# Linear attention, then a MoE layer, then a noisy top-2 MoE: the order of GpSimd's work in the attention is written out, low parts of weights are spread, and weight pieces are loaded sooner

## The chip, the cores and the metric

One core of one Trainium2 chip. The time is the device time of one launch in microseconds (us), as the median of several runs. The core has five engines that run beside each other and meet at semaphores: TensorE (PE, with its weight loads shown as PEld), VectorE (DVE), ScalarE (ACT), GpSimd (POOL) and SyncE (SP), whose queue issues nearly all DMAs here.

## The reference

Three layers in a row, all in float32 results:

```python
# attention: q, k, v of (4 batches, 8 heads, 576 tokens, 64), w_phi (64, 128)
phi(x) = concat[exp(p), exp(-p)],  p = x @ w_phi - max|x @ w_phi| per token
kv = phi(k)^T v ; z = sum over tokens of phi(k)
x  = (phi(q) @ kv) / (phi(q) @ z + 1e-6)          # -> (2304 tokens, 512)
# first MoE: w1, w2, w3 (512, 768), w_out (768, 512)
x  = max(x@w1, x@w2, x@w3) @ w_out
# second MoE: 8 experts, w1 (8, 512, 1024), w2 (8, 1024, 512)
noisy logits = x@w_gate + log(1+exp(x@w_noise)) * noise ; top 2 per token, softmax over the two
out[token] += weight * (relu(x[token] @ w1[e]) @ w2[e])
```

The weights of the first MoE arrive as 64-bit floats. The kernel turns their bits into float32 itself.

## The kernel before, in words

**The attention** runs over 16 steps s: a pair of heads of one batch each. Its work is a pipeline over periods a = 2 to 15 (function `period`), which holds three steps at once: step a is turned (transposed on PE), projected with w_phi, and its peaks and centers are made on DVE and its exponentials on ACT; step a-1 has kv_sum (PE, L525), z_sum (L544, with the key sums `zs`) and the turn of centered q; step a-2 has its denominator (PE L585, ACT `dn` L593, DVE turns and reciprocals L600 to L617) and its numerators (L570), which DVE divides into xT (L623). Even periods carry the 64 remaining tokens per head too (turn and projection "r").

**The key tiles**: `z_add(s)` on POOL adds the four tiles of the exponentials of k in three additions (zt twice, L534; zs, L535). z_sum on PE reads zs in the next period.

**The pieces**: the 64-bit weights of the first MoE are cut into 24 pieces of 512 KB (`halves`: group g = 0 to 2, matrix j, half c). Each period from a = 1 to 15 treats one piece (0 to 14); the others follow after the attention. A piece goes through:

- `narrow_load`: DMA of the bits on SP (L194) into a buffer `bits`, of which there are two
- `narrow_mid`: DVE takes the high word apart (L205, a tensor_scalar; L214, a scalar_tensor_tensor with two inputs), ACT makes the low word a number (L216); the result is `nm`
- `narrow_end`: ACT takes the absolute value (L224), POOL adds the low word to `nm` as integers (L225) and, for groups 0 and 1, masks tiny values (L228, L229); group 2 is masked on DVE in `narrow_mask` (L236)
- `narrow_out`: group 0 is split into a high part (ACT, L252) and a low part (L253, POOL for group 0, DVE for group 2), which the products of the first MoE read; group 1 is stored to DRAM (L247) and read again later (L258)

**What sets the order.** Every step is put on a plan with a due time (`at(t, f, ...)`, in units of about a us; a period is STEP = 10.9, the attention ends at T = 16 STEP), and the plan is run in the order of the times. For PE, ACT, DVE and SP this order is the order in the engine's queue. For POOL it is not: there the tile framework's scheduler orders the instructions by its own costs, unless an instruction is tied to the one before it by `in_order`. In the attention before the change nothing on POOL is tied.

**After the attention** the first MoE runs over 6 chunks of 384 tokens (PE L857 first products, L884 second), with the late pieces converted beside chunk 0; then routing, and the experts.

Of the kernel before, what the change touches and what calls it, by code (L numbers as in the profile page):

```python
# [9 lines left out]
F32 = mybir.dt.float32  # L10
F32R = mybir.dt.float32r
BF16 = mybir.dt.bfloat16
I32 = mybir.dt.int32
U32 = mybir.dt.uint32
AF = mybir.ActivationFunctionType
ALU = mybir.AluOpType
# [3 lines left out]
P = 128  # L20
TINY = 1.125 * 2.0 ** -15


class Plan:
# [5 lines left out]
    def at(self, t, f, *x):  # L30
        self.ops.append((t, len(self.ops), f, x))
# [7 lines left out]
def tile_linear_attention__then__moe__then__noisy_top2_moe(  # L39
# [20 lines left out]
    nc = tc.nc  # L60
# [30 lines left out]
    at = plan.at  # L91
    st, pools = {}, {}
# [36 lines left out]
    def split(hi, lo, src):  # L129
        nc.scalar.activation(hi, src, AF.Copy)  # L130
        nc.vector.tensor_tensor(lo, src, hi.bitcast(F32), op=ALU.subtract)  # L131

    xT = big.tile([P, KD, N], F32, name="xT", tag="big")

    def raw_tile():
# [5 lines left out]
    def ring(i):  # L141
        pool, n = (ring_a, 4) if i % 12 < 4 else (pools["ring_b"], 8)
        return tuple(pool.tile([P, 1024], F32R, name=nm, bufs=n) for nm in ("wh", "wl"))
# [5 lines left out]
    def block(ws, g, j):  # L149
        w = ws[j]  # L150
        if j < 3:
            return w[:, g * 256:(g + 1) * 256].rearrange("(a p) f -> p a f", p=P)
        return w[g * 256:(g + 1) * 256, :].rearrange("(a p) f -> p a f", p=P)

    def half(ap_, j, c):
        n = ap_.shape[1] // 2
        return ap_[:, c * n:(c + 1) * n, :]
# [5 lines left out]
    halves = [(g, j, c) for g in range(NG) for j in range(4) for c in range(2)]  # L163

    def direct(g, j):
        return g != 1
# [34 lines left out]
    def narrow_high(n):  # L201
        if ("bits", n) not in st:
            return
        m_ = pools["m2" if "m2" in pools else "attn"].tile([P, 512], I32, name="nm", tag="x2", bufs=3)
        nc.vector.tensor_scalar(m_, st["bits", n][:, :, 1], 0x07ffffff, 3, op0=ALU.bitwise_and,  # L205
                                op1=ALU.logical_shift_left)
        st["nh", n] = m_

    def narrow_low(n):
# [6 lines left out]
        nc.scalar.activation(low, low.bitcast(U32), AF.Copy, scale=float(2.0 ** -29))  # L216
        st["nm", n] = m_

    def narrow_end(n):
        if ("nm", n) not in st:  # L220
            return
        m_, bits = st["nm", n], st["bits", n]
        high = bits[:, :, 1].bitcast(F32)
        nc.scalar.activation(high, high, AF.Abs)  # L224
        nc.gpsimd.tensor_tensor(m_, m_, bits[:, :, 0], op=ALU.add)  # L225
        if halves[n][0] < 2:
            g_, o_ = bits[:, :, 0].bitcast(F32), m_.bitcast(F32)
            nc.gpsimd.tensor_scalar(g_, high, TINY, None, op0=ALU.is_ge)  # L228
            nc.gpsimd.tensor_tensor(o_, o_, g_, op=ALU.mult)  # L229

    def narrow_mask(n):
        if ("nm", n) not in st:
            return
        o_, bits = st.pop(("nm", n)).bitcast(F32), st.pop(("bits", n))
        if halves[n][0] == 2:
            nc.vector.scalar_tensor_tensor(o_, bits[:, :, 1].bitcast(F32), TINY, o_, op0=ALU.is_ge,  # L236
                                           op1=ALU.mult)
        st["nf", n] = o_

    def narrow_out(n):  # L240
        g, j, c = halves[n]
        if ("nf", n) not in st:
            return
        o_ = st.pop(("nf", n))
        if not direct(g, j):
            dst = half(block(narrow, g, j), j, c)
            dq.dma_start(dst, o_.rearrange("p (a f) -> p a f", a=dst.shape[1]))  # L247
            return
        if c == 0:
            W1[g, j] = ring(4 * g + j)  # L250
        hi, lo = (w[:, c * 512:(c + 1) * 512] for w in W1[g, j])
        nc.scalar.activation(hi, o_, AF.Copy)  # L252
        (nc.vector if g else nc.gpsimd).tensor_tensor(lo, o_, hi.bitcast(F32), op=ALU.subtract)  # L253

    def w1_load(g, j):
        src = block(narrow, g, j)
# [140 lines left out]
    kps, qps = {}, {}  # L397
# [131 lines left out]
    def z_add(s):  # L529
        t = ap.tile([P, 2, 2, 2, NF], F32, name="zt")  # L530
        z = ap.tile([P, 2, 2, NF], F32, name="zs")
        for h in range(2):
            hs = slice(2 * h, 2 * h + 2)
            nc.gpsimd.tensor_tensor(t[:, h], kps[s][:, 0, hs], kps[s][:, 1, hs], op=ALU.add)  # L534
        nc.gpsimd.tensor_tensor(z, t[:, :, 0], t[:, :, 1], op=ALU.add)  # L535
        st["zs", s] = z

    def z_sum(s):
# [87 lines left out]
    NS = B * HP  # L626
    STEP = 10.9
# [35 lines left out]
    def step_halves(a):  # L663

        def count(a):
            return min(a, 1)

        n = sum(count(i) for i in range(a))
        return range(n, n + count(a) if a < NS else len(halves))
# [14 lines left out]
            at(t + backs[n] + 0.5, divide, c, n)  # L684

    def narrow_steps(n, at, *times):
        for t, f in zip(times, (narrow_load, narrow_mid, narrow_end, narrow_mask, narrow_out)):
            at(t, f, n)

    def loads(a, at):  # L690
        if 0 < a < NS:
            at(0.0, fill, a)
            if a == 3:
                at(3.0, routing_loads)
            if a == 2:
                at(2.0, routing_consts)
            if a + 1 < NS:
                if a > 1:
                    at(0.0, load_main, a + 1)
                at(0.0, load_vals, a + 1)  # L700
            if a + 1 == 2 * HP:
                at(0.0, load_rest, 1)
        if a == 2 * HP:
            at(7.5, load_rest_v, 1)
        if a < NS:
            for n in step_halves(a):
                narrow_steps(n, at, 5.0, 9.9, 12.25, 16.5, 21.5)

    def period(a):
        base = a * STEP  # L710
# [2 lines left out]
        def at(t, f, *x):  # L713
            plan.at(base + t, f, *x)
# [28 lines left out]
        if even:  # L743
# [3 lines left out]
                at(4.83 + 0.01 * g, center, a, "r", g)  # L747
            for sg in range(2):
                at(9.5, exp_k, a, "r", 0, sg)
        at(7.6, z_add, a)  # L750
        both(7.4, "q", a, at)
        at(4.6, kv_sum, b)
        at(6.8, z_sum, b)
# [66 lines left out]
    T = NS * STEP  # L820
# [105 lines left out]
    def small(shape, name, dt=F32, bufs=2):  # L926
        return pools["work"].tile(shape, dt, name=name, bufs=bufs)

    scat = []

    def in_order(ins, but=()):

        if st["loop"]:
            return
        names = {o.ins.name for o in but}
        for i in reversed(nc.cur_bb.bb.instructions):
            if i.engine == ins.ins.engine and i is not ins.ins and i.name not in names:
                tc.add_manual_dep(ins.ins, i.name,
                                  mybir.DependencyInfo(mybir.DependencyClass.NoSync,
                                                       mybir.DependencyReason.DATA))  # L940
                return

    st["loop"] = False

    def route(c):

# [583 lines left out]
    END = clock[0] + 1.9  # L1530
    at(END, open_rest)
    at(END + 1.6, routing_split)
    late_ones = step_halves(NS)
    narrow_steps(late_ones[0], at, T - 4.0, T + 4.0, T + 5.5, T + 10.0, T + 11.5)
    for i, n in enumerate(late_ones[1:]):
        t = END + 2.0 + 2.6 * i
        narrow_steps(n, at, END + (0.01 * i if i < 5 else 2.6 * i - 1.0), t, t + 2.65, t + 5.0, t + 6.0)
    for i, (g, j) in enumerate(((1, 0), (1, 1), (1, 2), (1, 3))):
        t = END + 0.1 + i * 2.6
        at(max(t - 6.3, T + 9.0) if i < 2 else max(t - 6.3, END + 0.06), w1_load, g, j)  # L1540
# [64 lines left out]
    for c in range(NCHUNK):  # L1605
        if c == 1:
            for i, job in enumerate(jobs):
                t = clock[0] + 8.0 * i
# [55 lines left out]
    for n, (e, M, row0) in enumerate(units):  # L1664
# [9 lines left out]
        if seven(n):  # L1674
            for two in ((0, 1), (2, 3)):
                for q_ in ORDER7:
                    for f in two:
                        pe(2 * 3 * HN / 2400, product, n, e, q_, f)
                        d0, d = (-0.03, 0.01) if two[0] and q_ == ORDER7[-1] else (0.02, 0.44)
# [165 lines left out]
```

## Time and profile before

| | us |
|---|---|
| median of 3 runs | 977.56 (977.53 to 977.63) |
| profiled execution | 977.7 |
| its span | 976.1 |

| engine | busy us | share of the span |
|---|---|---|
| PE | 944.0 | 97% |
| DVE | 608.1 | 62% |
| POOL | 507.6 | 52% |
| ACT | 479.9 | 49% |

The shares are means over stages: the attention is the first 200 us, the first MoE begins at 195.58 us. In the rows below, times count from the start of the span. In a timeline, the first number is the start, the second the duration of the row's instructions together (in us; a row can merge several of one kind, given as x2, x16), then engine, source line, operation, what is written and read with its shape, and in brackets the idle time of the engine before the row and what ended it. In a table of stretches, each engine's busy time in the stretch is followed by its number of instructions; then come the granted clock of TensorE (1.00 is full), the share of the DMA engines' time and GB/s.

### The profile page before, as it was taken

Reading aid. Unit: us, or ns where it says so; the run is one execution under the profiler, and the core shown is the slowest. Engines: PE = TensorE matmul, PEld = TensorE weight load, DVE = VectorE, ACT = ScalarE, POOL = GpSimd, SP = SyncE. Lnnn points to the kernel's source line nnn. Section 1 sums busy time; section 2 is a strip of 40 time slices with the busy share of each in tenths; the row PEclk is TensorE's granted clock in tenths of the full one; section 3 lists DMA queues with packets and bytes.
Section 4 is the critical chain, followed back from the end, with each engine's and each line's share of the span. In section 5 each row is a group of like instructions: output and inputs, shape, how many; then the busy total and the mean of one; then the engine's idle time right before and its main releaser. Section 6 shows DMA issues by size and latency. Waiting matters only on the chain. (4 is left out here: it accounts for less than half of the span.)

```text
span 976.1 us, 18313 instructions
## 1 busy us (share of the span) xinstructions
PE 944.0 (97%) x6841; PEld 817.6 (84%) x6841; DVE 608.1 (62%) x1251; ACT 479.9 (49%) x1020; POOL 507.6 (52%) x562
## 2 busy tenths in 40 slices
PE   7999898997999999999999999999999999999997
PEld 5666666686899999999998889889897989889895
DVE  5799999978454453645355525556577765766641
ACT  5888877835343424333344414327363554636350
POOL 6678877634147473645232553237474655647252
PEclk9999999999999999999999999999999999999999
DMA  7475554262146666566515254828475665748312
GB/s 201 127 216 143 158 174 131 67 216 87 54 154 177 220 187 207 170 223 182 166 46 203 62 181 151 304 79 310 144 298 167 219 228 173 269 130 318 113 33 71
DMA packets 121580, 164.95 MB, mean 169 GB/s; under 512 B 35438, under 2 KB 83694, under 8 KB 121490
## 3 DMA queue, kind: packets, MB, share of 16 engines
q1 hardware_dynamic: 110002, 133.83, 43.1%
q0 software_dynamic: 10928, 29.62, 8.8%
q8 instruction: 54, 0.88, 0.4%
q14 instruction: 36, 0.29, 0.1%
q10 hardware_dynamic: 560, 0.33, 0.1%
HBM read 117.28 MB, written 47.05 MB: 168 GB/s over the span
## 5 line engine op out<-in xcount | busy, mean ns | idle before, releaser
L857 PE MATMUL s<-xh,wh 128*128 128x384 f32 x432 | 149.0, 345 | 6.5 <-DVE a L867 6.5
L857 PE MATMUL s<-xh,wl 128*128 128x384 f32 x432 | 145.8, 338 | 0.0
L857 PE MATMUL s<-xl,wh 128*128 128x384 f32 x432 | 145.6, 337 | 0.0
L1318 POOL DMA_INDIRECT out_dram<-o,emeta x40 | 47.1, 1178 | 129.1 <-DVE o L1316 62.3
L857 PEld LDWEIGHTS s<-xh,wh 128*128 128x128 f32 x432 | 81.5, 189 | 14.2 <-DVE a L867 7.6
L867 DVE TENSOR_TENSOR a<-s,a 128x384 f32<-128x384 f32 x72 | 39.9, 555 | 82.6 <-PE s L857 80.4
L1393 DVE TENSOR_TENSOR wl<-raw,wh 128x1024 fp32r<-128x1024 f32 x58 | 70.8, 1221 | 26.5 <-ACT wh L1385 25.8
L1308 PE MATMUL p<-wh,hh 128*128 128x512 f32 (+1 forms) x216 | 86.3, 400 | 0.0
L1308 PE MATMUL p<-wl,hh 128*128 128x512 f32 (+1 forms) x216 | 85.2, 395 | 0.0
L1308 PE MATMUL p<-wh,hl 128*128 128x512 f32 (+1 forms) x216 | 85.2, 394 | 0.0
L857 PEld LDWEIGHTS s<-xl,wh 128*128 128x128 f32 x432 | 81.6, 189 | 1.9 <-DVE xl L131 0.3
L857 PEld LDWEIGHTS s<-xh,wl 128*128 128x128 f32 x432 | 81.4, 188 | 0.0
L1385 ACT ACTIVATE wh<-raw 128x1024 fp32r<-128x1024 f32 x58 | 61.1, 1056 | 29.7 <-DMA raw<-in_moe_w_dram 15.4
L1033 POOL DMA_INDIRECT meta<-mt,si x36 | 37.0, 1028 | 52.5 <-DVE si L1029 43.4
L1361 POOL TENSOR_TENSOR raw<-raw 128x256 f32<-128x256 f32 x24 | 19.6, 818 | 83.3 <-DMA raw<-in_moe_w_dram 44.6
L1166 PE MATMUL s<-gx,wh 128*128 128x304 f32 x288 | 62.1, 302 | 0.0
L534 POOL TENSOR_TENSOR zt<-kp 128x512 f32<-128x512 f32 x32 | 41.4, 1314 | 37.8 <-ACT kp L484 37.8
L130 ACT ACTIVATE hh<-a 128x384 fp32r<-128x384 f32 x36 | 18.8, 522 | 85.6 <-DVE a L867 85.6
L131 DVE TENSOR_TENSOR gx<-t,gx 128x512 fp32r<-128x512 f32 (+3 forms) x82 | 39.4, 495 | 34.3 <-ACT gx L130 32.8
L130 ACT ACTIVATE gx<-t 128x512 fp32r<-128x512 f32 (+3 forms) x82 | 34.9, 447 | 45.3 <-DVE t L1141 27.8
L1095 POOL DMA_INDIRECT gx<-x2d,emeta x28 | 28.1, 1003 | 46.8 <-PE t L1105 17.1
L225 POOL TENSOR_TENSOR nm<-nm,bits 128x512 int32<-128x512 int32 x24 | 32.9, 1373 | 37.3 <-DVE nm L214 19.7
(315 smaller groups left out, 2655.8 us busy)
## 6 DMA issues: line engine op xcount, KB each, us to landing
raw<-in_moe_w_dram SPq DMA_DIRECT2D x58, 512.0 KB
raw<-in_moe_w_dram SPq DMA_DIRECT2D x48, 256.0 KB
sums<-qh SPq DMA_DIRECT2D x24, 512.0 KB
sums<-raw SPq DMA_DIRECT2D x24, 512.0 KB
wh<-sums SPq DMA_DIRECT2D x24, 512.0 KB
wl<-sums SPq DMA_DIRECT2D x24, 512.0 KB
bits<-in_moe_w_dram SPq DMA_DIRECT2D x18, 512.0 KB
out_dram<-zrow SPq DMA_DIRECT2D x9, 512.0 KB
```

The costliest lines, as they stand in the source:

```text
L130: nc.scalar.activation(hi, src, AF.Copy)
L131: nc.vector.tensor_tensor(lo, src, hi.bitcast(F32), op=ALU.subtract)
L225: nc.gpsimd.tensor_tensor(m_, m_, bits[:, :, 0], op=ALU.add)
L534: nc.gpsimd.tensor_tensor(t[:, h], kps[s][:, 0, hs], kps[s][:, 1, hs], op=ALU.add)
L857: nc.tensor.matmul(p_, a[:, d, fs], b_, start=(n == 0), stop=(n == 3 * KD - 1))
L867: nc.vector.tensor_tensor(a, p_, st.pop("a"), op=ALU.max)
L1033: ins = nc.gpsimd.indirect_dma_start(out=meta, out_offset=bass.IndirectOffsetOnAxis(ap=si[:, t, kk:kk + 1], axis=0), in_=mt[:, t, kk, :], ...
L1166: nc.tensor.matmul(bk["p"], a[:, d, fs], b_[:, d, :], start=(d == 0 and i == 0), stop=(d == 1 and i == 2))
L1308: nc.tensor.matmul(p_, a, b_[:, fw], start=(f == 0 and r == 0), stop=(f == (3 if seven(n) else F2 - 1) and r == 2))
L1318: alone(e, nc.gpsimd.indirect_dma_start(out=out, out_offset=bass.IndirectOffsetOnAxis(ap=mt[:m, i, 1:2], axis=0), in_=o[:m], in_offset=Non ...
L1385: nc.scalar.activation(WE[e, i][0], st["w2", e, i], AF.Copy)
L1393: nc.vector.tensor_tensor(wl, st.pop(("w2", e, i)), wh.bitcast(F32), op=ALU.subtract)
```

## The change

- `in_order` moves up in the function and is now used in the attention: the three additions of `z_add`, the integer addition, the mask on POOL and the low part of group 0 are each tied to the POOL instruction that stands before them in the plan.
- The integer addition becomes a step of its own, `narrow_add`, due right after `narrow_mid` (9.92 in the period); `z_add` is due at 9.95 instead of 7.6. So POOL has in each period: addition, zt, zt, zs, then (12.25, that is 1.35 into the next period) the mask.
- `narrow_out` of the eight pieces of group 0 is due at 10.0 of period 1 + a // 2 periods later, instead of 10.6 of the next period. Five `nm` buffers hold the pieces in the attention instead of three.
- `narrow_load` is due at 0.5 of the period instead of 5.0, and for the first piece at -2.9 of period 1.
- The piece of the last period has `narrow_mid`, addition and mask 2.0 later.
- The late pieces have their addition at t + 1.0, ahead of the absolute value (t + 2.65).

```diff
+    def narrow_add(n):
+        if ("nm", n) in st:
+            in_order(nc.gpsimd.tensor_tensor(st["nm", n], st["nm", n], st["bits", n][:, :, 0], op=ALU.add))
+
     def narrow_end(n):
...
-        m_, bits = st["nm", n], st["bits", n]
-        high = bits[:, :, 1].bitcast(F32)
-        nc.scalar.activation(high, high, AF.Abs)
-        nc.gpsimd.tensor_tensor(m_, m_, bits[:, :, 0], op=ALU.add)
-        if halves[n][0] < 2:
-            g_, o_ = bits[:, :, 0].bitcast(F32), m_.bitcast(F32)
-            nc.gpsimd.tensor_scalar(g_, high, TINY, None, op0=ALU.is_ge)
-            nc.gpsimd.tensor_tensor(o_, o_, g_, op=ALU.mult)
+        m_, bits = st.pop(("nm", n)).bitcast(F32), st.pop(("bits", n))
+        h_ = bits[:, :, 1].bitcast(F32)
+        nc.scalar.activation(h_, h_, AF.Abs)
+        if halves[n][0] == 2:
+            st["mask", n] = m_, h_
+            return
+        g_ = bits[:, :, 0].bitcast(F32)
+        in_order(nc.gpsimd.tensor_scalar(g_, h_, TINY, None, op0=ALU.is_ge))
+        in_order(nc.gpsimd.tensor_tensor(m_, m_, g_, op=ALU.mult))
+        st["nf", n] = m_
...
-            nc.gpsimd.tensor_tensor(t[:, h], kps[s][:, 0, hs], kps[s][:, 1, hs], op=ALU.add)
-        nc.gpsimd.tensor_tensor(z, t[:, :, 0], t[:, :, 1], op=ALU.add)
+            in_order(nc.gpsimd.tensor_tensor(t[:, h], kps[s][:, 0, hs], kps[s][:, 1, hs], op=ALU.add))
+        in_order(nc.gpsimd.tensor_tensor(z, t[:, :, 0], t[:, :, 1], op=ALU.add))
...
-        for t, f in zip(times, (narrow_load, narrow_mid, narrow_end, narrow_mask, narrow_out)):
+        for t, f in zip(times, (narrow_load, narrow_mid, narrow_add, narrow_end, narrow_mask, narrow_out)):
...
-                narrow_steps(n, at, 5.0, 9.9, 12.25, 16.5, 21.5)
+                d = 2.0 * (a == NS - 1)
+                narrow_steps(n, at, -2.9 if a == 1 else 0.5, 9.9 + d, 9.92 + d, 12.25 + d, 16.5, 21.5 if a > 8 else 10.0 + (1 + a // 2) * STEP)
...
-        at(7.6, z_add, a)
+        at(9.95, z_add, a)
...
-    narrow_steps(late_ones[0], at, T - 4.0, T + 4.0, T + 5.5, T + 10.0, T + 11.5)
+    narrow_steps(late_ones[0], at, T - 4.0, T + 4.0, T + 4.02, T + 5.5, T + 10.0, T + 11.5)
...
-        narrow_steps(n, at, END + (0.01 * i if i < 5 else 2.6 * i - 1.0), t, t + 2.65, t + 5.0, t + 6.0)
+        narrow_steps(n, at, END + (0.01 * i if i < 5 else 2.6 * i - 1.0), t, t + 1.0, t + 2.65, t + 5.0, t + 6.0)
```

## Rows read from the trace of the kernel before

**Rows 1.** Busy time of each engine by stretch (us, instructions), then clock and DMA.

```profile
93.13:116.66 23.53, 21.46 (x322) 15.56 (x322) 22.55 (x44) 19.91 (x54) 18.94 (x15) 1.00 0.57 165
34.00:195.58 161.58, 149.85 (x2217) 106.43 (x2209) 153.23 (x285) 133.10 (x351) 122.55 (x91) 0.98 0.50 146
195.58:260.00 64.42, 56.95 (x327) 50.43 (x324) 49.33 (x80) 26.77 (x46) 22.03 (x20) 0.97 0.35 115
260.00:960.00 700.00, 699.43 (x3939) 632.23 (x3938) 384.64 (x849) 298.08 (x572) 339.39 (x405) 1.00 0.55 181
```

**Rows 2.** Timeline of DVE: a piece's two bit instructions, in the attention and later.

```profile
93.13 1.23 DVE L205 TENSOR_SCALAR nm<-bits 128x512 int32<-128x512 int32 x1
94.39 1.66 DVE L214 SCALAR_TENSOR_TENSOR nm<-bits,nm 128x512 int32<-128x512 int32 x1
105.41 1.46 DVE L205 TENSOR_SCALAR nm<-bits 128x512 int32<-128x512 int32 x1
...
226.15 0.41 DVE L205 TENSOR_SCALAR nm<-bits 128x512 int32<-128x512 int32 x1
226.60 0.69 DVE L214 SCALAR_TENSOR_TENSOR nm<-bits,nm 128x512 int32<-128x512 int32 x1
```

**Rows 3.** Timeline of POOL over one even period of the attention.

```profile
92.80 2.71 POOL L534 TENSOR_TENSOR zt<-kp 128x512 f32<-128x512 f32 x2 [2.13 <-ACT kp L484]
95.58 1.61 POOL L535 TENSOR_TENSOR zs<-zt 128x512 f32<-128x512 f32 x1
97.16 1.28 POOL L225 TENSOR_TENSOR nm<-nm,bits 128x512 int32<-128x512 int32 x1
98.41 1.25 POOL L253 TENSOR_TENSOR wl<-nm,wh 128x512 fp32r<-128x512 f32 x1
99.64 1.58 POOL L228 TENSOR_SCALAR bits<-bits 128x512 f32<-128x512 f32 x1
101.30 1.31 POOL L229 TENSOR_TENSOR nm<-nm,bits 128x512 f32<-128x512 f32 x1
```

**Rows 4.** Timeline of PE over one pair of periods of the attention.

```profile
93.45 0.66 PE L416 MATMUL t<-ident,qm 128*128 128x128 f32 x4 [0.84 <-ACT dn L593]
...
98.88 0.46 PE L437 MATMUL s<-wphi,th 64*128 64x128 f32 x2 [0.84 <-DVE xT L623]
99.73 0.37 PE L437 MATMUL t<-wphi,th 64*128 64x128 f32 x1 [0.40 <-DVE xT L623]
...
100.37 1.93 PE L525 MATMUL k<-kp,vt 128*32 128x256 f32 x32
...
106.02 0.66 PE L416 MATMUL t<-ident,qm 128*128 128x128 f32 x4
...
110.44 1.93 PE L525 MATMUL k<-kp,vt 128*32 128x256 f32 x32
...
112.63 0.40 PE L544 MATMUL k<-zs,vt 128*32 128x128 f32 x8
...
116.99 0.66 PE L416 MATMUL t<-ident,qm 128*128 128x128 f32 x4 [0.83 <-ACT dn L593]
```

**Rows 5.** Timelines of SP, DVE and PE around the first piece, second period.

```profile
15.06 2.16 SPq L394 DMA_DIRECT2D vt<-in_v_dram  x2
17.26 0.62 SPq L194 DMA_DIRECT2D bits<-in_moe_w_dram  x1
...
22.37 0.43 DVE L205 TENSOR_SCALAR nm<-bits 128x512 int32<-128x512 int32 x1 [3.33 <-DMA bits<-in_moe_w_dram]
...
17.28 0.66 PE L416 MATMUL t<-ident,qm 128*128 128x128 f32 x4
19.19 0.52 PE L556 MATMUL s<-ident,kvT 128*128 128x128 f32 x3 [0.82 <-DVE dq L471]
23.59 1.11 PE L495 MATMUL t<-ident,dq 128*128 128x128 f32 x4 [3.22 <-ACT th L426]
28.86 1.93 PE L525 MATMUL k<-kp,vt 128*32 128x256 f32 x32
```

More of the change, by code (lines that the diff above doesn't have):

```diff
@@ L131, in split, with in_order @@
         nc.vector.tensor_tensor(lo, src, hi.bitcast(F32), op=ALU.subtract)
+    scat = []
+    def in_order(ins, but=()):
+        if st["loop"]:
+            return
+        names = {o.ins.name for o in but}
+        for i in reversed(nc.cur_bb.bb.instructions):
+            if i.engine == ins.ins.engine and i is not ins.ins and i.name not in names:
+                tc.add_manual_dep(ins.ins, i.name,
+                                  mybir.DependencyInfo(mybir.DependencyClass.NoSync,
+                                                       mybir.DependencyReason.DATA))
+                return
+    st["loop"] = False
     xT = big.tile([P, KD, N], F32, name="xT", tag="big")
@@ L203, in narrow_high @@
             return
-        m_ = pools["m2" if "m2" in pools else "attn"].tile([P, 512], I32, name="nm", tag="x2", bufs=3)
+        m_ = pools["m2" if "m2" in pools else "attn"].tile([P, 512], I32, name="nm", tag="x2", bufs=3 if "m2" in pools else 5)
         nc.vector.tensor_scalar(m_, st["bits", n][:, :, 1], 0x07ffffff, 3, op0=ALU.bitwise_and,
@@ L221, in narrow_end @@
             return
-        m_, bits = st["nm", n], st["bits", n]
-        high = bits[:, :, 1].bitcast(F32)
-        nc.scalar.activation(high, high, AF.Abs)
-        nc.gpsimd.tensor_tensor(m_, m_, bits[:, :, 0], op=ALU.add)
-        if halves[n][0] < 2:
-            g_, o_ = bits[:, :, 0].bitcast(F32), m_.bitcast(F32)
-            nc.gpsimd.tensor_scalar(g_, high, TINY, None, op0=ALU.is_ge)
-            nc.gpsimd.tensor_tensor(o_, o_, g_, op=ALU.mult)
-    def narrow_mask(n):
[L232 to L238, printed above, removed]
+        m_, bits = st.pop(("nm", n)).bitcast(F32), st.pop(("bits", n))
[3 more added lines that the diff above has]
+            st["mask", n] = m_, h_
+            return
+        g_ = bits[:, :, 0].bitcast(F32)
+        in_order(nc.gpsimd.tensor_scalar(g_, h_, TINY, None, op0=ALU.is_ge))
+        in_order(nc.gpsimd.tensor_tensor(m_, m_, g_, op=ALU.mult))
+        st["nf", n] = m_
+    def narrow_mask(n):
+        if ("mask", n) in st:
+            st["nf", n], h_ = st.pop(("mask", n))
+            nc.vector.scalar_tensor_tensor(st["nf", n], h_, TINY, st["nf", n], op0=ALU.is_ge, op1=ALU.mult)
     def narrow_out(n):
@@ L252, in narrow_out @@
         nc.scalar.activation(hi, o_, AF.Copy)
-        (nc.vector if g else nc.gpsimd).tensor_tensor(lo, o_, hi.bitcast(F32), op=ALU.subtract)
+        if g:
+            nc.vector.tensor_tensor(lo, o_, hi.bitcast(F32), op=ALU.subtract)
+        else:
+            in_order(nc.gpsimd.tensor_tensor(lo, o_, hi.bitcast(F32), op=ALU.subtract))
     def w1_load(g, j):
@@ L927, in small @@
         return pools["work"].tile(shape, dt, name=name, bufs=bufs)
[L929 to L943, printed above, removed]
     def route(c):
```

## The prediction

> **What bounds the kernel now.** I read the stages first [rows 1]. From 260 us to 960 us TensorE (PE) is busy 699.43 of 700 us at full clock: nothing that the change touches can shorten that part, and whatever the attention ends earlier reaches the end of the kernel, if the stage between (195.58 to 260) does not give it back. The attention from 34.00 to 195.58 is different: PE is busy 149.85 of 161.58 us and VectorE (DVE) 153.23, so DVE is the fuller engine. The reader is to see in the last row, one pair of periods (even and odd, 23.53 us), that DVE is busy 22.55, ScalarE (ACT) 19.91, GpSimd (POOL) 18.94 and PE 21.46: DVE has nothing left, PE has 2.07.
>
> Then I looked for where PE's 2.07 us sit [rows 4]. They are three waits per pair: 0.84 for `dn` (ACT) at the head of the even period, 0.84 and 0.40 for `xT` (DVE) in its middle, and the 0.83 at 116.99 is the first of the next pair. Between 100.37 and 110.44, kv_sum to kv_sum, nothing waits: 10.07 us, and nearly all intervals of that half measure the same to 0.01 us whatever DVE does meanwhile. That is PE's own pace there. The other half is 23.53 - 10.07 = 13.46 with the waits, 11.4 without; a pair that waits for nothing takes 21.47 instead of 23.53.
>
> Then why DVE is full [rows 2]. The two instructions that turn a weight piece's bits (L205, L214) take 1.23 to 1.46 and 1.66 us in the attention. The same shapes take 0.41 and 0.69 at 226 us, where POOL does nothing beside them. In the attention they start while POOL adds the key tiles (zt, zs: 92.80 to 97.19) [rows 3]: L205 is let go about when the first zt ends, L214 about when the second ends, and zs, which then comes third, takes 1.61. So they wait for POOL rather than work: per pair 1.23 + 1.46 + 2 x 1.66 = 6.01 us against 2 x (0.41 + 0.69) = 2.20, an excess of 3.8 us on the engine that is full. Everything else that DVE does in a period (`den` turns, peaks, centers) shows no such stretching beside POOL.
>
> **The change part by part.** *The order on POOL.* Now POOL does zt, zt, zs, then the piece's integer addition (L225), the low part, the mask (L228, L229). After the change the addition stands first and the key tiles behind it. The addition reads what L214 writes, so POOL cannot start the key tiles before L214 is done: L205 and L214 no longer meet them. Worth: up to 3.8 us of DVE per pair. PE can take only its 2.07. What is late next is nothing on DVE (18.75 of 21.47), and ACT (19.91 of 21.47) has 1.56 left.
>
> *What it delays.* `zs` comes later, and PE's z_sum waits for it. From the end of L214: addition 1.28, two zt 2.5 (1.25 each, what the low part of the same shape takes in [rows 3]; in the row they take 2.71 beside DVE), zs about 1.3: 5.1 us; I take 5.2. When does L214 end? DVE now starts L205 0.32 before PE's turn of q in the even period, and 0.61 before it in the odd one (105.41 against 106.02). A period sheds 1.9 us of DVE and some 1.0 of PE, so L205 moves about 0.9 further ahead: 1.2 to 1.5 before the turn, L214's end 1.1 later, `zs` 4.8 to 5.1 after the turn. z_sum stands 112.63 - 106.02 = 6.6 after it in the odd period, and later in the even one, which has two turns and a projection more. So about 1.5 us of slack: cost nothing. Without this cover (L214 ending where it does now, some 2.5 us after the odd turn) `zs` would land 7.7 after the turn, 1.1 too late.
>
> *The low parts (L253) spread wider.* Eight POOL subtractions of 1.25 us and eight ACT copies run in other periods, none less. POOL's chain is 1.28 + 2.5 + 1.3 + 1.25 + 1.58 + 1.31 = 9.2 us where a low part stands in it, 8.0 where none does, against 10.7 a period: it fits. Two more `nm` buffers hold the pieces meanwhile; they issue nothing.
>
> *Loads.* Piece loads move from 5.0 to 0.5 into the period. On SP this passes other DMAs in two periods only. In the first, the load (at 17.26 now) goes ahead of the two value loads (issued from 15.06) [rows 5], 2.2 us sooner; these come 0.6 later and are needed a period later. There DVE waits 3.33 us and, through ACT, PE 3.22 for exactly this piece. In the third, the load passes fourteen small routing loads and spares a later wait of the same kind, which is inside the sum below. Turn of q to kv_sum takes 28.86 - 17.28 = 11.58 us at the start, and 100.37 - 93.45 - 1.24 = 5.68 when nothing waits. The 0.82 us at 19.19 (for `dq`) stays, and I leave 0.7 for a landing still slightly late: 7.2. Gain 4.4. If the 2.2 us sooner is all that it brings, 2.2; if nothing is late, 5.1.
>
> *The last piece of the attention* goes 2 us later, behind DVE's turns of the denominator; its excess vanishes or stays (at most 2 us, once), and PE has other work there: 0, bounds -1 and +1.
>
> *The late pieces (195.58 to 260).* Their addition is put before ACT's absolute value, in the order POOL already keeps. PE idles 64.42 - 56.95 = 7.5 us here for conversions that all follow the end of the attention: 0, bounds -2 and +2.
>
> **Sum.** From 34.00 to 195.58 PE's idle time is 161.58 - 149.85 = 11.7 us, and a mean granted clock of 0.98 (levels 1.0 and 0.5, that is 2.4 and 1.2 GHz) takes 0.02 x 161.58 = 3.2 more; a PE that never waits should keep its clock. Together 15.0. Not all small waits go when every engine runs close: I leave 0.2 us in each of 13 periods, 2.6. So 15.0 - 2.6 + 4.4 = 16.8 us off the profiled execution's 977.7 (span 976.1 and 1.6 around it): 960.9. The median shown is 977.56, 0.1 lower: **960.8 us**. Its own range: 957 (no waits left) to 965.
>
> **Two rules weighed.** That L205 and L214 take two to three times as long beside POOL is shown in [rows 2, 3]. The Trainium skill ("SBUF — State Buffer", "Who interferes with whom") says that the ports shared by VectorE and GpSimd are an exclusive lock, held for a whole instruction, and that issue order decides who blocks. By that rule, with which the trace agrees (L205 1.23, alone 0.41), a fixed order can move the collision instead of removing it, and the time would be that of the first rival below. On PE, the row of a pair has weight loads busy for 15.56 of 23.53 us, matmuls for 21.46 [rows 1]. The Trainium skill ("Perfetto Trace Analysis", "Identifying the Most-Contended Engine") says that matmul busy time does not tell how near TensorE is to its limit and that weight-load busy time does. By that rule PE would have room below 21.47 and the time would be that of the last rival; the unchanging 10.07 speaks against it.
>
> **The rivals.**
> *The collision moves to the mask.* With POOL's chain at 8.0 to 9.2 of 10.7 us, L205 may start while POOL still does the mask of the piece before (1.31 us, L229) and wait for it. For: little idle time on POOL. Against: the addition cannot start before L214, so at most one such wait fits into a period, and DVE has slack. Price: 1.3 us in each period, 2.6 a pair; relief is 3.8 - 2.6 = 1.2 instead of the 2.07 that PE needs; 6.5 pairs x 1.2 = 7.8, and 4.4: 977.6 - 12.2 = 965.4. If part is also given back between 195.58 and 260 (up to 4 us more): 969.
>
> *Slower: z_sum waits for `zs`.* POOL is one queue now: if the addition is late (for L214, for ACT's L216, for a load), the key tiles are late with it, and behind z_sum stand PE's denominator and numerators, ACT's `dn`, DVE's `den` turns. Price: 1.1 us in 7 odd periods as worked out, 7.7, less 4.4 at the start: 981; and 988 if the even ones pay as much, once DVE falls back by what PE loses. It decides if L214 ends more than 6.6 - 5.2 = 1.4 us after the turn of q. Against: that needs L214 to stay as late as today with its collision gone.
>
> *It does not do what it says.* The first piece lands no sooner, because the transfers ahead of it set when it lands and not its issue, and L205 and L214 are slow for another reason than POOL's key tiles (a strided tile, a wait that the view does not show): nothing moves, 977.6. Against: they are fast at 226 us, on tiles of the same stride.
>
> *Faster still.* PE is not at its pace at all; then ACT's 19.91 a pair is next: (21.47 - 19.91) x 6.5 = 10.1 us more: 951.
>
> **How the numbers follow.** What a measurement of this kernel can tell from no change is about 0.2%, 2 us. Forecast 0.62; collision moves, with or without something given back, 0.23; slower 0.07; does not do what it says 0.05; faster still 0.03. Faster by over 0.2% (below 975.6): 0.62 + 0.23 + 0.03 = 0.88; within 0.2%: 0.05; slower: 0.07. The range takes the forecast with its bounds at both ends of the stage between (955.5) and most of the first rival: 955.5 to 970.
>
> **What would show it.** L205 at about 0.41 and L214 at about 0.69 in the attention, POOL's additions ahead of zt; kv_sum to kv_sum 10.07 and about 11.4 in turn; no wait of PE for `xT` or `dn`; the first L205 near 19.5 instead of 22.37; kv_sum of the second period near 24.5. Wrong: L205 at 1 us or more beside L228 or L229; PE idle before L544 for `zs`; a longer stretch from the first product of the next stage to 260.

## The result, and the profile after

The changed kernel takes 954.92 us (median of 4 runs, 954.43 to 956.06) against 977.54 (977.20 to 977.63): a ratio of 0.977, interval 0.9754 to 0.9788. The forecast was 960.8 with a range from 955.5: right in sign and in the mechanism of the gain, 5.9 us too small, and the time lies 0.6 below the range. The profiled execution took 955.07, its span is 953.5, that is 22.6 less than before.

The changed file has other line numbers. L221 and L230 are the bit instructions (L205 and L214 before), L237 is the integer addition (L225), L249 and L250 the mask (L228, L229), L274 the low part (L253), L555 and L556 the key tiles (L534, L535), L546 kv_sum (L525), L565 z_sum (L544), L437 the turns on PE (L416), L458 the projections (L437) and L516 the turns of the centered values (L495). Mind L437, which stands for different work in the two.

Where the time came from is read off the starts of kv_sum (first row of L525 before, L546 after) and of the first product of the next stage (L857, L879):

| stretch | before | after | gain | forecast |
|---|---|---|---|---|
| start to kv_sum of the second period | 28.86 | 24.98 | 3.9 | 4.4 |
| 13 intervals kv_sum to kv_sum behind it | 154.08 | 134.96 | 19.1 | 12.4 |
| last of these to the first product | 12.64 | 12.64 | 0.0 | 0 |
| first product to the end of chunk 0 (its last L884, L906) | 66.82 | 66.58 | 0.2 | 0 |
| the rest of the span | 713.70 | 714.34 | -0.6 | 0 |

This is one profile of each kernel. In two further profiles of the changed kernel kv_sum of the second period stands at 24.21 and 24.78, so the 3.9 is known to about 0.8.

The stretches that answer to [rows 1]: a pair of periods from kv_sum to kv_sum, the attention, the stage behind it, the rest (busy time of PE, PEld, DVE, ACT, POOL with instructions; clock, DMA share, GB/s).

```profile
66.77:87.36 20.59, 20.59 (x324) 15.12 (x323) 19.38 (x43) 19.31 (x53) 17.81 (x14) 1.00 0.68 188
30.12:172.58 142.46, 142.41 (x2216) 103.45 (x2208) 133.02 (x286) 132.62 (x351) 120.98 (x91) 1.00 0.58 165
172.58:239.16 66.58, 60.49 (x338) 54.35 (x335) 49.92 (x80) 28.45 (x49) 23.24 (x21) 0.95 0.34 111
240.00:940.00 700.00, 699.18 (x3938) 632.08 (x3937) 384.29 (x849) 295.88 (x568) 339.71 (x406) 1.00 0.55 181
```

PE fills the attention: 142.41 of 142.46 us at clock 1.00, where it had 149.85 of 161.58 at 0.98. The pair takes 20.59 us instead of 23.53. PE's busy time in the attention fell by 7.4 us although its work is the same. Part of that is TensorE's clock. Before, two of the seven odd intervals take 11.75 and 11.76 instead of 10.07: behind the waits of the even half the granted clock fell to 0.5, for 3.41 us each time, and kv_sum itself took 3.59 and 3.10 us instead of 1.93.

```profile
123.91 3.59 PE L525 MATMUL k<-kp,vt 128*32 128x256 f32 x32
...
171.18 3.10 PE L525 MATMUL k<-kp,vt 128*32 128x256 f32 x32
```

Two times 3.41 us at half clock make 3.4 of the 7.4. The other 4.0, and the fall from 21.46 to 20.59 in a pair whose clock is 1.00 in both, is the clue to what the forecast missed; it comes back below.

DVE's two bit instructions, which answer to [rows 2], in an even and an odd period:

```profile
81.11 0.44 DVE L221 TENSOR_SCALAR nm<-bits 128x512 int32<-128x512 int32 x1
81.58 0.69 DVE L230 SCALAR_TENSOR_TENSOR nm<-bits,nm 128x512 int32<-128x512 int32 x1
92.48 0.42 DVE L221 TENSOR_SCALAR nm<-bits 128x512 int32<-128x512 int32 x1
92.94 0.69 DVE L230 SCALAR_TENSOR_TENSOR nm<-bits,nm 128x512 int32<-128x512 int32 x1
```

They have within 0.03 us the durations that they had at 226 us before. POOL beside them, which answers to [rows 3]:

```profile
79.95 1.31 POOL L250 TENSOR_TENSOR nm<-nm,bits 128x512 f32<-128x512 f32 x1
82.51 1.30 POOL L237 TENSOR_TENSOR nm<-nm,bits 128x512 int32<-128x512 int32 x1 [1.24 <-ACT bits L232]
83.77 2.52 POOL L555 TENSOR_TENSOR zt<-kp 128x512 f32<-128x512 f32 x2
86.36 1.27 POOL L556 TENSOR_TENSOR zs<-zt 128x512 f32<-128x512 f32 x1
87.59 1.28 POOL L274 TENSOR_TENSOR wl<-nm,wh 128x512 fp32r<-128x512 f32 x1
88.84 1.64 POOL L249 TENSOR_SCALAR bits<-bits 128x512 f32<-128x512 f32 x1
90.56 1.30 POOL L250 TENSOR_TENSOR nm<-nm,bits 128x512 f32<-128x512 f32 x1
```

The mask of the piece before ends at 81.26, L230 starts at 81.58 and ends at 82.27, the addition starts at 82.51 and the key tiles follow it. zs ends 5.15 after the turn of q (82.48), in time for z_sum.

PE over the same pair, which answers to [rows 4], has no row with a wait:

```profile
66.77 1.93 PE L546 MATMUL k<-kp,vt 128*32 128x256 f32 x32
...
72.41 0.65 PE L437 MATMUL t<-ident,qm 128*128 128x128 f32 x4
...
76.84 1.93 PE L546 MATMUL k<-kp,vt 128*32 128x256 f32 x32
...
82.48 0.66 PE L437 MATMUL t<-ident,qm 128*128 128x128 f32 x4
...
87.36 0.85 PE L546 MATMUL k<-kp,vt 128*32 128x256 f32 x12
```

The odd half is 10.07 as before, the even half 10.52. All six even intervals behind 34 us are 10.90, 10.74, 10.52, 11.05, 10.74 and 10.52: the excess over 10.52 is 1.35 us in all. Part of it is the collision that the first rival named. In odd periods whose POOL chain has a low part the mask comes late enough to meet L230 (POOL and then DVE around 40 us):

```profile
36.63 1.28 POOL L274 TENSOR_TENSOR wl<-nm,wh 128x512 fp32r<-128x512 f32 x1
37.88 1.64 POOL L249 TENSOR_SCALAR bits<-bits 128x512 f32<-128x512 f32 x1
39.60 1.50 POOL L250 TENSOR_TENSOR nm<-nm,bits 128x512 f32<-128x512 f32 x1
```

```profile
39.50 0.42 DVE L221 TENSOR_SCALAR nm<-bits 128x512 int32<-128x512 int32 x1
39.95 1.68 DVE L230 SCALAR_TENSOR_TENSOR nm<-bits,nm 128x512 int32<-128x512 int32 x1
...
102.66 0.77 DVE L221 TENSOR_SCALAR nm<-bits 128x512 int32<-128x512 int32 x1 [0.85 <-DMA bits<-in_moe_w_dram]
```

L230 takes 1.68, 1.70 and 1.70 us at 39.95, 60.76 and 123.28. The fourth long interval (11.05) starts with a load that landed 0.85 late, at 102.66.

The opening, which answers to [rows 5] (SP, then DVE, then PE):

```profile
15.27 1.61 SPq L210 DMA_DIRECT2D bits<-in_moe_w_dram  x1
```

```profile
20.41 0.79 DVE L221 TENSOR_SCALAR nm<-bits 128x512 int32<-128x512 int32 x1 [1.42 <-DMA bits<-in_moe_w_dram]
21.23 1.64 DVE L230 SCALAR_TENSOR_TENSOR nm<-bits,nm 128x512 int32<-128x512 int32 x1
```

```profile
19.13 0.52 PE L577 MATMUL s<-ident,kvT 128*128 128x128 f32 x3 [0.82 <-DVE dq L492]
21.60 0.66 PE L516 MATMUL t<-ident,dq 128*128 128x128 f32 x4 [1.30 <-ACT th L447]
```

The piece is issued 2.0 us sooner and L221 starts 2.0 sooner (20.41 against 22.37, forecast 19.5). PE's wait of 3.22 is 1.30, and the turns behind it start 1.99 sooner (21.60 against 23.59).

That is only half of the 3.9 us. Before, the granted clock fell to 0.5 during PE's wait and stayed there from 21.6 to 28.4 us; after, it stays at 1.00. The work from these turns to kv_sum therefore took 5.27 us before (28.86 - 23.59) and takes 3.38 after (24.98 - 21.60): the other 1.9. A stretch of the opening before and one after, with the clock third from the right:

```profile
20.00:30.00 10.00, 6.78 (x72) 5.66 (x74) 3.44 (x8) 7.17 (x19) 6.38 (x5) 0.66 0.78 246
17.28:30.00 12.72, 10.51 (x159) 7.63 (x161) 9.68 (x16) 10.89 (x29) 8.04 (x6) 1.00 0.89 253
```

The same fall stands in the openings of e1 and e4 below, where PE waits 2.45 and 2.13 us there, and in none of the runs with the sooner load.

### The profile page after: what moved, and what is told of

The parts are those of the page before. It is cut to its first block, busy times and chain, and to the rows that moved or that the text cites. A ratio compares the mean times of both kernels' runs of the same rounds, so it can differ in the third digit from the quotient of the medians.

```text
span 953.5 us, 18302 instructions
## 1 busy us (share of the span) xinstructions
PE 935.4 (98%) x6841; PEld 814.2 (85%) x6841; DVE 589.0 (62%) x1251; ACT 479.2 (50%) x1020; POOL 505.1 (53%) x562
## 5 line engine op out<-in xcount | busy, mean ns | idle before, releaser
L879 PE MATMUL s<-xh,wh 128*128 128x384 f32 x432 | 149.5, 346 | 5.0 <-DVE a L889 5.0
L879 PE MATMUL s<-xh,wl 128*128 128x384 f32 x432 | 146.6, 339 | 0.0
L879 PE MATMUL s<-xl,wh 128*128 128x384 f32 x432 | 146.4, 339 | 0.0
L879 PEld LDWEIGHTS s<-xh,wh 128*128 128x128 f32 x432 | 82.2, 190 | 12.2 <-DVE a L889 7.5
L879 PEld LDWEIGHTS s<-xl,wh 128*128 128x128 f32 x432 | 82.1, 190 | 1.5
L879 PEld LDWEIGHTS s<-xh,wl 128*128 128x128 f32 x432 | 82.1, 190 | 0.0
L237 POOL TENSOR_TENSOR nm<-nm,bits 128x512 int32<-128x512 int32 x24 | 33.5, 1395 | 51.8 <-DVE nm L230 22.6
L1323 DVE SCALAR_TENSOR_TENSOR o<-p,emeta,pv 128x512 f32<-128x512 f32 (+1 forms) x27 | 20.2, 748 | 47.2 <-PE p L1315 41.2
```

The lines of the kernel that those rows point to most:

```text
L237: in_order(nc.gpsimd.tensor_tensor(st["nm", n], st["nm", n], st["bits", n][:, :, 0], op=ALU.add))
L879: nc.tensor.matmul(p_, a[:, d, fs], b_, start=(n == 0), stop=(n == 3 * KD - 1))
```

## The experiments

The kernels ran in four sets, each with its own runs of the kernel before on the same chip: 977.90 us (e1 to e4), 977.83 (e5, e6, e8), 976.57 (e7, e9) and 978.68 (e10). In the second and third the changed kernel itself ran again: 954.39 (after_again; ratio 0.9759, 0.9741 to 0.9777) and 954.97 (after_third; 0.9773, 0.9751 to 0.9795). Differences of times below are within a set; intervals are those of kv_sum to kv_sum in one profile of each kernel. The last piece's 2 us and the order of the late pieces were not run alone; the stretches in which they stand changed by 0.0 and 0.2 us.

My theory before them: DVE's excess beside the key tiles is all that kept PE waiting; PE's own pace is 20.6 us a pair and not 21.47; the loads pay in the opening. The rival: the pace is 21.47 as forecast, and another part of the change (loads, spread, a written-out order as such) brought the rest.

**e1: the order alone.** The changed kernel with loads and low parts due as before.

```diff
-narrow_steps(n, at, -2.9 if a == 1 else 0.5, 9.9 + d, 9.92 + d, 12.25 + d, 16.5, 21.5 if a > 8 else 10.0 + (1 + a // 2) * STEP)
+narrow_steps(n, at, 5.0, 9.9 + d, 9.92 + d, 12.25 + d, 16.5, 21.5)
```

> The changed kernel with the piece loads due at 5.0 of the period and the low parts one period later, as before; only GpSimd's order is changed. Theory (the order alone removes DVE's excess and with it nearly all of PE's waits in the attention; the loads bring the opening's 3.9 us): the gain falls from 22.6 to 18.7 us, so 958.8 us (957.5 to 960), kv_sum of the second period back near 28.9, the 13 intervals behind it still about 135 us. Rival A (the earlier loads also keep the pieces in time in the later periods): intervals sum to 139 or more and the time is 963 or more. Rival B (the prediction's sizes: pair at 21.47, 0.2 us left in each period): 965.

959.90 us, ratio 0.982 (0.9776 to 0.9859): 18.0 us of gain. kv_sum of the second period is at 28.70, the 13 intervals sum to 136.55 (theory 135, rival A from 139). One of them is long, 12.39 at 38.92: there the load stands behind the routing loads on SP (issued at 42.00) and DVE waits 3.06 us for it. Behind it the even intervals are 11.09, 10.69, 10.68, 10.52 and 10.51. So the order is the main part. (Five `nm` buffers and the later last piece are in it too.)

**e2: the loads alone.** The kernel before with one number of it changed.

```diff
-narrow_steps(n, at, 5.0, 9.9, 12.25, 16.5, 21.5)
+narrow_steps(n, at, -2.9 if a == 1 else 0.5, 9.9, 12.25, 16.5, 21.5)
```

> The kernel before with only the piece loads moved to 0.5 of the period (-2.9 for the first); GpSimd's order, the low parts and the late pieces as before. Theory: the opening gains its 3.9 us (kv_sum of the second period near 25.0 instead of 28.86), the 13 intervals behind it stay near 154 us, since DVE stays full: 973.6 us (972.5 to 975). Rival A (the loads matter in every period): intervals shorten by 3 us or more, 970 or less. Rival B (the opening's gain is lost again, since DVE and GpSimd meet as before and the attention's end is set by them): within 1 us of 977.5.

974.28 us, ratio 0.9968 (0.9949 to 0.9987): 3.6 us. kv_sum of the second period is at 24.33; the first five even intervals stay at 13.45 to 13.52, with L205 at 1.23 and L214 at 1.66 (40.62, 41.88). The theory holds. Together, 18.0 and 3.6 make 21.6 of the 22.6. The remaining 1.0 is less than the intervals of the two can tell (4 and 1.9 us either way). The profiles show one such term: the third period's load costs 1.9 in e1 (12.39 against 10.5) and only 0.9 in the kernel before (14.36 against 13.46), where DVE was late anyway.

**e3: the same written-out order, but tiles first.** One number of the changed kernel.

```diff
-        at(9.95, z_add, a)
+        at(7.6, z_add, a)
```

> The changed kernel with one number changed: the key tiles' additions are due at 7.6 of the period instead of 9.95, so GpSimd's order is written out as before, but the tiles stand ahead of the piece's addition. Theory (what pays is which instruction GpSimd does beside DVE's two bit instructions): L221 is again over 1 us and L230 near 1.65 in every period, the intervals kv_sum to kv_sum return to 23.5 us a pair, and only the opening's gain stays: 973 us (970 to 976). Rival A (any fixed order of GpSimd, and earlier loads, bring the gain): 955 to 958. Rival B (a fixed order with the tiles first is worse than the scheduler's): above 979.

972.49 us, ratio 0.9948 (0.9932 to 0.9965), as the theory had it: about e2's time (974.28), and all even intervals but one are 13.46 to 13.54. (The one, 11.96, stands behind an odd interval of 11.74 at half clock, as in the kernel before.) DVE, then POOL, in one even period of it:

```profile
100.37 1.42 DVE L221 TENSOR_SCALAR nm<-bits 128x512 int32<-128x512 int32 x1
101.81 1.65 DVE L230 SCALAR_TENSOR_TENSOR nm<-bits,nm 128x512 int32<-128x512 int32 x1
```

```profile
98.96 2.53 POOL L555 TENSOR_TENSOR zt<-kp 128x512 f32<-128x512 f32 x2 [1.44 <-ACT kp L505]
101.57 1.35 POOL L556 TENSOR_TENSOR zs<-zt 128x512 f32<-128x512 f32 x1
103.60 1.30 POOL L237 TENSOR_TENSOR nm<-nm,bits 128x512 int32<-128x512 int32 x1 [0.68 <-issue]
```

L221 starts while the second zt runs and L230 while zs runs. So a fixed order by itself is worth nothing that shows beside the loads' gain; what pays is that the addition, which waits for L230, stands ahead of the tiles.

**e4: the kernel before without the tiles.** No order written out, loads as before.

```diff
     def z_add(s):
+        if s:
+            st["zs", s] = st["zs0"]
+            return
```

> The kernel before without the key tiles' additions on GpSimd (zt, zs) for all steps but the first, whose key sums are used for every step; this leaves out part of the computation (the denominators are those of wrong sums, and later routing may differ). GpSimd's order is otherwise left to the scheduler, loads as before. Theory (the additions beside DVE's bit instructions are all that keeps PE waiting, and PE's own pace is 20.6 us a pair): L205 about 0.41 and L214 about 0.69, the intervals kv_sum to kv_sum of a pair 20.6 to 20.8, the first product of the next stage at 176 to 177.5 us. Rival A (the prediction: PE's own pace is 21.47 a pair): the first product at 181 or later. Rival B (other GpSimd work, the addition and the mask, then meets the bit instructions as before): a pair above 22.5, the first product at 188 or later.

961.01 us, ratio 0.9825 (0.9785 to 0.9865). A pair of its intervals:

```profile
115.10 1.93 PE L525 MATMUL k<-kp,vt 128*32 128x256 f32 x32
...
125.18 1.93 PE L525 MATMUL k<-kp,vt 128*32 128x256 f32 x32
...
135.69 1.93 PE L525 MATMUL k<-kp,vt 128*32 128x256 f32 x32
```

```profile
120.14 0.42 DVE L205 TENSOR_SCALAR nm<-bits 128x512 int32<-128x512 int32 x1
120.60 0.69 DVE L214 SCALAR_TENSOR_TENSOR nm<-bits,nm 128x512 int32<-128x512 int32 x1
```

10.08 and 10.51: a pair takes 20.59 with another edit than the change. Rivals A and B fall. The first product stands at 178.98, outside the 176 to 177.5 that I expected, because the third period has its late load here too (an interval of 14.54: L205 waits 4.30 us, PE 2.17, and the clock then falls to 0.5 for 3.41).

**e5: more work on PE.** The turns of k twice from step 3 on.

```diff
-            nc.tensor.transpose(pt[:, j, :], src, ident)
+            for _ in range(2 if kind == "k" and s > 2 else 1):
+                nc.tensor.transpose(pt[:, j, :], src, ident)
```

> The changed kernel with more work on PE alone: the turns of k's tiles are done twice from step 3 on (the second writes the same values), by the rows some 0.44 us of PE in each of 13 periods. Theory (PE sets the attention's pace now, in both halves of a pair): all intervals longer by about 0.44, in sum 5.5 to 6 us, 960.7 us. Rival (another engine or a chain of waits sets the pace, and PE only looks full): under 2 us more, below 957.

958.29 us, 3.9 above the changed kernel's 954.39: neither figure. The intervals say why. All are 10.51 (odd) and 10.95 (even), each 0.44 longer than the floor of the changed kernel, and none has any excess left. Four L230 still take 1.68 to 1.70 (at 39.64, 60.85, 103.77 and 125.23), but PE does not wait for them: a slower PE gives the other engines the time that they lacked. So the 13 intervals grow by 4.6 (139.27 against 134.65), not by 5.7. From the first product to the end of chunk 0 the time is then 2.1 us shorter (65.34 against 67.44; mean granted clock between 178 and 240 us 1.00 against 0.94). In the attention the theory holds: PE sets the pace in both halves.

```profile
67.53:88.99 21.46, 21.46 (x332) 15.98 (x331) 19.12 (x43) 19.55 (x54) 17.71 (x15) 1.00 0.62 167
```

**e6: more work on DVE.** One peak of q twice from step 3 on.

```diff
-        nc.vector.tensor_reduce(m, st["pj", kind, g][:, :n], axis=AX.X, op=ALU.max,
-                                apply_absolute_value=True)
+        for _ in range(2 if kind == "q" and g == 1 and s > 2 else 1):
+            nc.vector.tensor_reduce(m, st["pj", kind, g][:, :n], axis=AX.X, op=ALU.max,
+                                    apply_absolute_value=True)
```

> The changed kernel with more work on DVE alone: one peak of q is taken twice from step 3 on, 0.6 to 0.7 us of DVE in each of 13 periods. Theory (DVE has about 1.8 us of room a pair at the pace of 20.6): 0 to 3 us more, 955 to 958, the even intervals longer by at most 0.4. Rival (DVE sets the pace now as it did before): 13 x 0.65 = 8.4 us more, 963.

960.96 us, 6.6 above the changed kernel: a miss of the theory, nearer to the rival. The odd intervals stay at 10.07, the even ones are 11.17 to 11.79. The pair without a collision:

```profile
68.16:89.40 21.24, 21.10 (x323) 15.29 (x323) 20.19 (x45) 19.49 (x53) 17.19 (x14) 1.00 0.63 175
```

DVE is busy 20.19 of 21.24 us, and yet its timeline has no row with idle time there: its rows leave small gaps between them (in the changed kernel's second run a row of L638 ends at 75.27 and the next row starts at 75.37). The extra peak costs 0.73 a period (9.98 from one L221 to the next instead of 9.25). So if DVE sets the pace of this pair, its own pace in the changed kernel is, as an estimate, 21.25 - 2 x 0.73 = 19.8 a pair, not the sum of its rows, and its room below PE's 20.59 is 0.8 and not 1.8. Two engines stand within 4% of each other.

**e7: low parts together.** The changed kernel with `narrow_out` at 21.5 for every piece.

```diff
-... 16.5, 21.5 if a > 8 else 10.0 + (1 + a // 2) * STEP)
+... 16.5, 21.5)
```

> The changed kernel with the low parts due one period after their piece, as before the change, so that eight periods in a row hold one each. Theory (spreading them is worth nothing on the whole, because e1_order_only, which has them so, shows excess over 10.5 of 0.59, 0.19 and 0.18 in its later even intervals, about as much as the changed kernel): within 1 us of it, 953.5 to 955.5. Rival (the spread is what leaves GpSimd the time to keep the order): 2 us or more above it, 956.5.

954.71 us beside 954.97: the spread of the low parts, as the change has it, is worth nothing that can be measured.

**e8, e9, e10: low parts where POOL has time.** The period in which each of the eight low parts is due was chosen (the lists are those of the three kernels), and the load of period 9 issued sooner. The diff has names where the kernels have the numbers.

```diff
-                narrow_steps(n, at, -2.9 if a == 1 else 0.5, 9.9 + d, 9.92 + d, 12.25 + d, 16.5, 21.5 if a > 8 else 10.0 + (1 + a // 2) * STEP)
+                narrow_steps(n, at, {1: -2.9, 9: -3.5}.get(a, 0.5), 9.9 + d, 9.92 + d, 12.25 + d, 16.5,
+                             OUT if a > 8 else 10.0 + (PERIOD[a - 1] - a) * STEP)
# e8:  OUT = 18.0, PERIOD = (3, 5, 7, 8, 11, 13, 14, 15)
# e9:  OUT = 21.5, PERIOD = (3, 5, 7, 8, 9, 11, 13, 14)
# e10: OUT = 21.5, PERIOD = (3, 5, 7, 8, 9, 10, 11, 13)
```

> The changed kernel with seven of the eight low parts moved to other periods (so that all but the one near 98 us stand in periods that also turn the remaining tokens, where GpSimd has more time), group 1's pieces stored 3.5 sooner, and the load of the piece of period 9 issued 4.0 sooner. Theory (what the even intervals still have over 10.5 is the mask's multiplication beside L230 in three periods, 0.24 to 0.40 each, and one late load): all even intervals 10.50 to 10.56, 1.2 to 1.5 us faster than the changed kernel: 953.5 us. Rival A (the excess is not from the low parts, but from GpSimd's chain as such): the same intervals keep their excess, 954.9. Rival B (the later low parts make the first products wait, since the last of them ends beside the attention's end): 956 or more.

961.20 us, 6.8 slower than the changed kernel in the same set. The excess of the first intervals is gone as expected (10.51, 10.52, 10.52), but one interval is 13.87: five `nm` buffers don't hold that many pieces, and L221 waits for a store to end.

```profile
113.63 0.43 DVE L221 TENSOR_SCALAR nm<-bits 128x512 int32<-128x512 int32 x1 [1.43 <-DMA narrow<-nm]
...
125.49 0.43 DVE L221 TENSOR_SCALAR nm<-bits 128x512 int32<-128x512 int32 x1 [2.52 <-DMA narrow<-nm]
```

> As e8_low_even, but with times for the low parts that leave a free nm buffer in every period (group 1's pieces stored when the changed kernel stores them): five low parts in periods with remaining tokens, and two near 98 and 108 us. Theory (e8's one long interval of 13.87 was a wait for a buffer, and the mask beside L230 is all that is left of DVE's excess): no interval above 10.8, at most one of them above 10.55, first product 0.5 to 1.0 us sooner than in the changed kernel: 953.6 us. Rival (the low parts' place does not matter on the whole, what is won in the intervals is lost behind the attention, as in e8, where the first product stood 0.5 later behind the last interval): 954.4 or more.

956.23 us (955.55 to 956.71), 1.3 above the 954.97 of the changed kernel, whose runs reach from 954.10 to 956.61: the intervals are as the theory has them (all even ones 10.51 or 10.52 but one of 10.74; 133.85 in sum against 134.74), and the rival wins on the whole. The low part at 160.21 pushes zs, and PE's z_sum of the last period waits for it (the weight loads' row):

```profile
168.46 0.16 PEld L565 LDWEIGHTS k<-zs,vt 128*32 128x32 f32 x8 [0.78 <-POOL zs L556]
```

The first product is only 0.2 sooner, and the stage behind it is 1.1 us longer (67.68 against 66.61; the three profiles of the changed kernel have 66.58, 67.44 and 66.61).

> As e9_low_even5, with the last low part where the changed kernel has it (period 13) and no low part later, since in e9 the one at 160.21 pushed zs back and z_sum of the last period waited 0.78 us for it. Theory (the low parts' place pays as long as none stands in the last two periods): the first even intervals without excess (10.52 each, against 10.95 and 10.73 in the changed kernel), no wait of z_sum, first product 0.5 to 0.9 us sooner than its 172.15, and 954.2 us. Rival (the late pieces' loads then land as late as in e9, and the stage after the attention gives it all back): 955 or more.

955.68 us (953.70 to 956.59), ratio 0.977 (0.9753 to 0.9786): not told apart from the changed kernel; the theory's 954.2 is missed, as its rival had it. In its profile, the fastest execution of the five, the first even intervals are 10.51 as expected, but a later one is 10.99; the wait of z_sum is gone, and the first product stands at 171.65, 0.5 before that of after_third and 0.15 behind that of after_again. Nothing that I tried beats the changed kernel by more than can be measured.

## Why the prediction missed

**What held.** The mechanism, step by step: L205 and L214 at 0.41 and 0.69 (but for the collisions named below), the addition ahead of zt, no wait for `xT` or `dn`, 10.07 in the odd half, no wait for `zs`, nothing lost at the last piece or in the stage behind (66.58 against 66.82). The clock term held too: 3.2 us forecast, 3.4 found (two falls of 3.41 us to half), and after the change the clock stays at 1.00 throughout the attention. e3 and e4 show that the place of the tiles is the cause, and e2 that the loads bring only a small part (3.6 us). The first rival did come, in three of six even intervals (excess 0.38, 0.22 and 0.22, with L230 at 1.68 to 1.70), and cost 0.8 us in all. The rule of the Trainium skill that I weighed ("SBUF — State Buffer", "Who interferes with whom") says that the shared ports are an exclusive lock and that the order of issue decides who blocks. e3 agrees with it: the same additions, only issued ahead of L221 and L230, bring these back to 1.42 and 1.65.

**The step that failed: "The other half is 23.53 - 10.07 = 13.46 with the waits, 11.4 without; a pair that waits for nothing takes 21.47 instead of 23.53."** The measured even half without waits is 10.52 (after; 10.51 in e4), a pair 20.59. The term is mis-sized by 0.88 a pair. In the sum it is the 11.7 us of PE's idle time. The 13 intervals before take 154.08 us where the pace, 7 x 10.07 + 6 x 10.52, is 133.6: 20.5 us lost, 3.4 of them at half clock, so the waits cost 17.1 and not 11.7. This is the whole step: 5.4 us too little. I had taken PE's waits from the idle times of its matmul rows (0.84 + 0.84 + 0.40, about 2.07), and took all that these rows call busy for work. But starts tell more than idle times. From turn of q to kv_sum the kernel before takes 100.37 - 93.45 = 6.92 us [rows 4], after 87.36 - 82.48 = 4.88: 2.04 lost where the rows of before show 1.24. From kv_sum to the turn it is 0.91 (6.55 against 5.64). Together 2.95. The weight loads of before show part of what the matmul rows hide (the idle time in brackets):

```profile
93.45 0.42 PEld L416 LDWEIGHTS t<-ident,qm 128*128 128x128 f32 x4 [1.37 <-ACT dn L593]
...
98.85 0.29 PEld L437 LDWEIGHTS s<-wphi,th 64*128 64x128 f32 x2 [1.00 <-ACT qp L504]
99.73 0.18 PEld L437 LDWEIGHTS t<-wphi,th 64*128 64x128 f32 x1 [0.59 <-DVE xT L623]
...
106.01 0.42 PEld L416 LDWEIGHTS t<-ident,qm 128*128 128x128 f32 x4 [0.47 <-ACT bits L216]
```

0.47 stands at every turn of q, also where nothing is late, after the change too; so the waits here are 0.90 + 1.00 + 0.59 = 2.49, nearer to 2.95 than 2.07, still short of it. The difference may be the tail of each broken stream: the same product's row lasts 0.27 us while its successor starts 0.11 later (PE after the change), so a row in front of a gap counts up to 0.16 of the gap as busy, and the row before `xT` counts more.

```profile
86.82 0.27 PE L458 MATMUL t<-wphi,th 64*128 64x128 f32 x1
...
86.93 0.27 PE L458 MATMUL t<-wphi,th 64*128 64x128 f32 x1
```

That the tails make up all of the remaining 0.46 is argued, not shown. That the pace is 20.59 is shown three times: after, e4, and e5, where 0.44 of added work lengthens each half by 0.44. That the hidden part is real shows after the change too: the 13 intervals exceed the pace by 1.35 us, and PE's rows there show 0.05 us of idle time.

**The reason that I gave against it** was "the unchanging 10.07". It was sound for the odd half at full clock (five of the seven; the other two ran partly at half clock) and said nothing of the even one, the half with all the waits. The Trainium skill ("Perfetto Trace Analysis", "Identifying the Most-Contended Engine") says that matmul busy time does not tell how near TensorE is to its limit. The trace agrees, since PE's busy time in a pair fell from 21.46 to 20.59 with the same work. The Trainium skill (same page and section) also names weight-load busy time, beside the share of peak arithmetic, as the better measure of room. Here weight loads are busy for 15.12 of 20.59 us, and e5 shows that this sequence of products has no room all the same; the measurement decides. My last rival let PE fall to ACT's 19.91 and had a chance of 0.03; the truth lay between it and the forecast.

**The smaller terms.** The 2.6 us left for small waits measured 1.4: 1.2 more gain. The clock term was 0.2 short. The opening gave 3.9 instead of 4.4: 0.5 less, which the 0.8 between profiles of the changed kernel covers. The forecast had put it down to the wait alone; half of it is the clock. The end of the span gave back 0.4. In sum 5.4 + 1.2 + 0.2 - 0.5 - 0.4 = 5.9, the miss.

**What e6 corrects beside it.** The forecast had DVE at 18.75 of 21.47, with nothing late next. By the estimate from e6, DVE's own pace is about 19.8 of 20.59. The conclusion held, by a margin of 0.8 us.

## What to carry to other kernels

When an engine holds up its neighbour, as POOL's key tiles did DVE's bit instructions here (0.42 and 0.69 us without them in e4, 1.42 and 1.65 beside them in e3), look for an instruction of the first that already depends on the victim's result, and put it ahead of the offender in that engine's queue. The dependence then keeps the two apart. POOL stands idle for it (1.24 us before the addition at 82.51), which cost nothing here; a fixed order with the tiles ahead (e3) brought none of this. To size what a stall is worth, measure from start to start against a stretch of the same work without the stall. Of 2.95 us lost in a pair, the weight loads' idle time showed 2.49 and the matmul rows' 2.07, so both were lower bounds. And read the granted clock of a stretch before its length is put down to waits. And add work to each engine in turn after a gain: it told here that PE sets the pace and that DVE is about 0.8 us behind, which the sums of busy time did not.

## What the runs showed that I had not expected

A slightly slower engine can hide what others lose: with 0.44 us more of PE in each period (e5) no even interval is above 10.95, although four L230 still meet the mask, so a fifth of the added time came back in the attention. Behind it e5 needs 65.34 us from the first product to the end of chunk 0, against 66.58, 67.44 and 66.61 in the three profiles of the changed kernel and 67.98 in e6. e5's mean granted clock from 178 to 240 us was 1.00, and 0.94 and 0.97 in the changed kernel's second profile and in e6 (the levels are 1.0 and 0.5). What sets the clock in that stage was not tried.

A wait may cost twice. Before the change the granted clock fell to 0.5 once in the opening and twice in the attention, each time in a wait of PE or right behind one; after it, the first fall comes at 205 us, behind the attention. The fall at 124 us cost little all the same: the even half behind it takes 11.95 and not 13.47, so the two together take 23.70, near the 23.53 at which DVE held every pair. Why only two of the six even halves with waits were followed by a fall is not shown.
